# A long convolution and a spectral mixing layer on one core: the identity read with the first constants, two zero columns left out, and the first transform's tiles shared anew between two engines

## The chip, the cores and the metric

The kernel runs on one core of a Trainium2 chip. A core has TensorE (matrix products, into the banks of PSUM), VectorE (DVE in the profile), ScalarE (ACT), GpSimd (POOL) and SyncE (SP). DMA transfers are issued here by SP and POOL and carried out by 16 DMA engines. The metric is the time of one execution in device microseconds; before the change the median of three runs was 385.36 us (384.66 to 386.22).

## The reference

Two layers in a row, with x of shape (8, 5696, 128) and h of shape (5696, 128): a causal convolution along the sequence, by FFT, and then a mixing of the 64 lowest frequencies with complex 128 x 128 matrices, followed by a gated residual.

```python
# first layer
Xf = np.fft.rfft(x, n=2 * S, axis=1)
Hf = np.fft.rfft(h, n=2 * S, axis=0)
u0 = np.fft.irfft(Xf * Hf[None], n=2 * S, axis=1)[:, :S, :]
# second layer
X = np.fft.rfft(u0, axis=1)
Y = np.zeros_like(X)
Yr = Xr @ w_r - Xi @ w_i          # the first 64 modes, one matrix each
Yi = Xr @ w_i + Xi @ w_r
u = u0 + np.fft.irfft(Y, n=S, axis=1)
out = u + np.maximum(u @ w_ch, 0.0)
```

## The kernel before

The kernel is written instruction by instruction. A recorder (line 21) keeps one list for each engine; an instruction's waits come from tokens that it reads and writes, and each engine runs its own list strictly in the order in which the program adds to it. So does each DMA queue (SP's and POOL's).

**The transform.** S = 5696 is split into NQ = 89 rows of J = 64 positions. The first transform goes along the 89 rows and gives NK = 90 frequencies k, real and imaginary part: one matmul with the moving matrix `F1` of 2 * NK = 180 columns for each feature d. Of these, the imaginary parts at k = 0 and k = 89 are zero for every input. `a_tile` (line 461) makes four features: four matmuls into two PSUM banks, and then one evacuation (`evac`, line 304) of 128 x 720 values to `As` in fp16, as a multiplication by 1/64, on VectorE (line 317) or on ScalarE (line 313). 32 such tiles make `As` for one pair of batches; the same is done for h at half the width (`Ah`). The second transform (`second`, line 606, and `filter_tick`, line 486, for h) takes four k in a tick; for each k and each batch it adds two matmuls, one with the real and one with the imaginary part.

**The four passes.** The eight batches go in four pairs g_ = 0 to 3. The body of a pass has 23 ticks of four k (`tick`, line 650): second transform, products with the filter (`products`), a matmul pair W1/W2, evacuation to a slot of `Zs`/`Zt` on ScalarE, a store of the slot to the scratch `zscr` through SP's queue, and the matmuls with `G` that collect the 64 modes. In the last pass a slot is used again after eight ticks (NZL = 8): the evacuation of tick 21 writes the slot of tick 13, and so waits until the store of tick 13 has landed.

**The borders.** Between two passes all of `As` is made anew. Tiles j = 0 to 5 are spread over the last ticks (`border`, line 556: five on VectorE, one on ScalarE); tiles 6 to 31 follow in a loop (line 740). That loop takes the PSUM slots 4, 6, 0, 2 in turn, so a tile can start when the tile four places ahead of it has been evacuated. Odd tiles go to VectorE, even ones to ScalarE, the last one is halved between both. `second` of the next pass needs all 32 tiles.

**The opening.** For the first pass the tiles stand alone in a loop (line 717), with `eng=None`, which lets ScalarE and VectorE take turns; six ticks of the filter's second transform (`filter_tick`) are put between them, five of them evacuated by ScalarE and one by VectorE. `keep(16, ...)` after it is sixteen matmuls without use that keep TensorE busy. The opening cannot start before the first pair of x has been loaded through POOL's queue.

**The last pass and the tail.** While the last pass runs, a table `early` (line 557) issues the loads for the final stage at given ticks: POOL reads the weights `W`, the tables `S4b`, `S4a` and `IBs` and the first stored spectra `ZT0`, `ZT1`. At tick 14 it calls `load_id` (line 568): SP reads the 128 x 128 identity into `Id`, which lies on one of the buffers `R`. It is issued after ZY, that is after everything that read or wrote slots 8 and 9, the landing of their stores to `zscr` among it. The stores of ticks 13, 14 and so on stand behind it in SP's queue. The identity is used once, in eight transposes (line 824) in the tail, after the mixing matmuls. The tail (`u_z`, `mix`, `u_c`, from line 760) and the final stage (`u_tile`, `o_tile`) follow.

```python
early = {..., 11: lambda: load_zt(0, "gpsimd"),
         14: lambda: (load_id(), clear_zt(1)), ...}
def load_id():
    dma("sync", id_sb[:, :], bass.AP(c_w, 2 * P, [[3 * P, P], [1, P]]), "c", (), [("id",)], after=ZY)
```

Of the kernel before, what the change touches and what calls it, by code (L numbers as in the profile page):

```python
# [123 lines left out]
def bass_long_conv_fft__then__afno_spectral_mix_kernel(nc, x, h, moe_w_r, moe_w_i, moe_w_ch, out):  # L124
# [16 lines left out]
    fwd = np.exp(-2j * np.pi * np.outer(qq, kk) / (2 * NQ))  # L141
    f1 = np.zeros((P, 2 * NK))
    f1[0:NQ] = np.stack([fwd.real, fwd.imag], axis=2).reshape(NQ, 2 * NK)
    mat = np.exp(-2j * np.pi * (pp[:, None, None] * kk[None, :, None] / L + pp[:, None, None] * pp[None, None, :] / J))
# [64 lines left out]
    def take(nbytes):  # L209
# [38 lines left out]
          [at(f"Zt{i}", 1024, F16, a_g + GW * 2 + i * 2048) for i in range(NZX - NZ)]  # L248
    f1_sb = at("F1", 2 * NK, F16, take(2 * NK * 2))
    wc_sb = at("Wc", 2 * P, F16, take(2 * P * 2))  # L250
# [11 lines left out]
              (a_m2, a_g)]  # L262
    assert 2 * S + 8 * ZP <= AW * 2
    zt = [[at(f"ZT{i}{'ab'[p_]}", ZP, F16, zt_off[i][p_]) for p_ in range(2)] for i in range(NC)]
# [17 lines left out]
    c_sb = at("C", B * P, F16, a_x + 4 * S)  # L282
    id_sb = at("Id", P, F16, r_off[1])

# [14 lines left out]
    def bank(i):  # L299
        return ("bank", i)  # L300
# [45 lines left out]
    zf = x_sb[J:P, :].bitcast(F32)  # L346
    R.add("scalar", lambda e: e.copy(zf, ap(f1_sb, 2 * NK, J, P - J, 1, [[0, XW // 2]])), [("f1",)], [("xz",)])
    h_parts = [part for i in range(2) for part in (
# [67 lines left out]
    dma("sync", sg_sb[:, :], c_sg.ap(), "c", (), [("sg",)])  # L416
    dma("sync", wc_sb[:, :], bass.AP(c_w, 0, [[3 * P, P], [1, 2 * P]]), "c", (), [("wc",)])

    def mtok(k):
# [12 lines left out]
    for i in range(WARM):  # L432
        mm(pv(6 + i % 2, 0, [[1, 2 * NK]]), f1_sb[:, 0:P], f1_sb[:, :], True, True, [("f1",)], [bank(6 + i % 2)])

# [5 lines left out]
    for j in range(16):  # L440
        t = turns("h", [0, 2, 4])
        for i in range(4):
            d = 4 * j + i
            mm(pv(t + i // 2, (i % 2) * 2 * NK, [[1, 2 * NK]]),
               ap(hp_sb, 2 * J * HS, 0, P, d, [[HS, 2 * J]]), f1_sb[:, :], True, True,
               [("hz",), ("hp", d // DC), ("f1",)], [bank(t + i // 2)])
        for i in range(4 if j < 15 else 26):
            mm(pv(6 + i % 2, 0, [[1, 2 * NK]]), f1_sb[:, 0:P], f1_sb[:, :], True, True, [("f1",)], [bank(6 + i % 2)])
        evac(bass.AP(ah_sb, 4 * j, [[HW, P], [DH, 2 * NK], [2, 2], [1, 2]]),
             pv(t, 0, [[1, 2 * NK], [512, 2], [2 * NK, 2]]),  # L450
             [bank(t), bank(t + 1)], [("ah", j)], 1.0 / 64,
             eng="vector" if j in (3, 7) else "scalar")
# [8 lines left out]
    def a_tile(j, slots, eng=None):  # L461
        t = turns("s", slots) if len(slots) > 1 else slots[0]
        for i in range(4):
            d = 4 * j + i
            mm(pv(t + i // 2, (i % 2) * 2 * NK, [[1, 2 * NK]]),
               ap(x_sb, XW, 0, P, d, [[XS, 2 * J]]), f1_sb[:, :], True, True,
               XIN + XZ + [("f1",)], [bank(t + i // 2)])
        if eng == "both":
            for i, e in enumerate(("vector", "scalar")):
                evac(bass.AP(a_sb, 4 * j + 2 * i, [[AW, P], [D, 2 * NK], [1, 2]]), pv(t + i, 0, [[1, 2 * NK], [2 * NK, 2]]),  # L470
                     [bank(t + i)], [("as", j + i)], 1.0 / 64, eng=e, after=once(("hp", j), HP))
            return
        evac(bass.AP(a_sb, 4 * j, [[AW, P], [D, 2 * NK], [2, 2], [1, 2]]),
             pv(t, 0, [[1, 2 * NK], [512, 2], [2 * NK, 2]]),
             [bank(t), bank(t + 1)], [("as", j)], 1.0 / 64, eng=eng, after=once(("hp", j), HP))


    def xtok(n):
# [7 lines left out]
    def filter_tick(t, banks):  # L486
        n = len(ticks[t])
        hb = banks
        for i, k in enumerate(ticks[t]):
            for r in range(2):  # L490
                for dh in range(2):
                    mm(pv(hb[dh], i * DH, [[1, DH]]),
                       ap(m_sb, MW, J * dh, J, k * 3 * J + (J if r == 0 else 0) + dh * J, [[1, P]]),
                       ap(ah_sb, HW, J * dh, J, (2 * k + r) * DH, [[1, DH]]), r == 0, r == 1,
                       AHT + mtok(k) + [("ag", k)], [bank(hb[dh])])
# [54 lines left out]
    def load_s4(part):  # L550
# [24 lines left out]
    def keep(n, b0):  # L575
        for i in range(n):
            mm(pv(b0 + i % 2, 0, [[1, 2 * NK]]), f1_sb[:, 0:P], f1_sb[:, :], True, True, [("f1",)], [bank(b0 + i % 2)])

# [27 lines left out]
    def second(g_, t):  # L606
        sl = slot_of(g_, t)
        for i, k in enumerate(ticks[t]):
            for r in range(2):
# [231 lines left out]
    def o_tile(g_, b, r4):  # L841
# [97 lines left out]
```

## Time and profile before

| what | us |
|---|---|
| median of three runs (lowest, highest) | 385.36 (384.66, 386.22) |
| the profiled execution | 387.21 |
| its span, first to last instruction | 385.1 |
| TensorE busy | 362.4 (94%) |
| ScalarE busy | 314.3 (82%) |
| VectorE busy | 296.6 (77%) |
| GpSimd busy | 85.2 (22%) |
| granted TensorE clock, mean over the span | 0.98 |

The profile tells when each engine was busy and who ended each wait. A row of the groups gives the line of the program, the engine, the operation, out<-in, how often it ran, its busy time and mean duration in ns, and then the idle time of the engine just before it and what ended it. In a row of the timeline, the first number is the start and the second the length in us of a run of like instructions (xN); the bracket gives the idle time before it. TensorE is busy nearly throughout, but a matmul's recorded time overlaps that of the next, so the share alone does not say that TensorE is the limit. That has to be read stage by stage:

| stretch, us | stage |
|---|---|
| 0 to 27 | loads, transform of h |
| 27 to 43.5 | opening: first transform of pass 0, first ticks of the filter |
| 43.5 to 91, 107 to 147, 162 to 202, 218 to 262 | the bodies of the four passes |
| 91 to 107, 147 to 162, 202 to 218 | the three borders |
| 262 to 274 | tail: last spectra, mixing, transposes |
| 274 to 385 | final stage and output |

### The profile page before, as it was taken

To read this page: it belongs to the slowest core of one execution; us is meant where nothing else is said; L and a number is where in the kernel's file an instruction comes from. 1 tells how busy PE (TensorE), PEld (TensorE's weight loads), DVE (VectorE), ACT (ScalarE), POOL (GpSimd) and SP (SyncE) were. 2 spreads that over 40 slices of the span, in tenths; PEclk is the share of its full clock that TensorE was granted. 3 is DMA by queue.
4 is the path that set the end of the run, shared out by engine and by line. 5 is a ranking of instruction groups with operands and counts; after the bars stand their busy time and mean duration, and the time that the engine had idled before them with its cause. 6 is when DMAs were issued, how large, how long until landed. Compare 5 with 4: busy or idle time off the path is not lost.

```text
span 385.1 us, 12438 instructions
## 1 busy us (share of the span) xinstructions
PE 362.4 (94%) x5346; PEld 280.7 (73%) x5346; DVE 296.6 (77%) x336; ACT 314.3 (82%) x491; POOL 85.2 (22%) x134
## 2 busy tenths in 40 slices
PE   7989899999989999999999899978999999999994
PEld 7878766667856667756667666648789989888873
DVE  3649899988988998989999988761537767766665
ACT  8469699898989997899998899965447777688884
POOL 8812012100733311823203213307200000000000
PEclk9999999999999999999999999995799999999999
DMA  7999969977999995999995799999999999999877
GB/s 148 206 298 354 243 139 249 250 220 222 97 126 215 249 268 151 132 134 232 243 274 114 95 325 357 327 367 292 392 391 362 367 416 403 419 405 383 325 293 316
DMA packets 87137, 103.94 MB, mean 270 GB/s; under 512 B 22819, under 2 KB 72611, under 8 KB 83527
## 3 DMA queue, kind: packets, MB, share of 16 engines
q1 hardware_dynamic: 62603, 67.76, 50.7%
q0 software_dynamic: 24480, 35.40, 44.2%
q8 instruction: 42, 0.69, 0.7%
q14 instruction: 12, 0.10, 0.1%
HBM read 70.61 MB, written 51.12 MB: 316 GB/s over the span
## 4 chain that ended last, share of the span: by engine, by line
PE 76%; DMA 8%; DVE 6%; ACT 4%; POOL 3%; issue 2%; DVEq 0%; ACTq 0%; POOLq 0%
PE ps L323 76%; DMA Xr<-in_x_dram 4%; DMA zscr<-Zs 3%; DVE As L317 2%; DVE U L630 2%; POOL Xr L320 2%; ACT As L313 2%; ACT R L871 1%; POOL Hin L320 1%; DVE Xin L365 1%; DVE Hs L315 1%; ACT Zt L311 1%; ACT Zs L311 0%; DMA Hs<-Hs 0%; ACT Xs L311 0%
## 5 line engine op out<-in xcount | busy, mean ns | idle before, releaser
L323 PE MATMUL ps<-U,Wc 128*128 128x512 f16 (+1 forms) x368 | 94.4, 377 | 4.2 <-ACT Zs L311 3.7
L638 DVE TENSOR_TENSOR U<-Xs,Hs 128x2048 f16<-128x2048 f16 (+1 forms) x73 | 86.9, 1192 | 13.8 <-ACT Xs L311 13.1
L311 ACT CAST Xs<-ps 128x1024 f16<-128x1024 f32 (+1 forms) x77 | 75.1, 979 | 12.6 <-PE ps L323 7.6
L311 ACT CAST Zs<-ps 128x512 f16<-128x512 f32 (+1 forms) x132 | 69.3, 592 | 5.5 <-DMA zscr<-Zs 3.8
L872 DVE TENSOR_TENSOR O<-ps,R 128x512 f32<-128x512 f32 x81 | 52.3, 685 | 20.1 <-ACT R L871 11.2
L317 DVE TENSOR_SCALAR As<-ps 128x720 f16<-128x720 f32 x70 | 57.7, 886 | 5.2 <-PE ps L323 4.6
L871 ACT ACTIVATE R<-ps 128x512 f32<-128x512 f32 (+1 forms) x92 | 50.5, 591 | 8.5 <-PE ps L323 8.4
L323 PE MATMUL ps<-F,Xin 128*128 128x180 f16 x512 | 53.7, 249 | 3.9 <-DVE Xin L365 2.6
L323 PE MATMUL ps<-As,M 64*128 64x128 f16 x1440 | 50.3, 217 | 3.5 <-DVE U L630 2.9
L323 PEld LDWEIGHTS ps<-F,Xin 128*128 128x128 f16 x512 | 44.4, 155 | 12.6 <-DVE As L317 2.8
L323 PEld LDWEIGHTS ps<-U,Wc 128*128 128x128 f16 x368 | 28.6, 97 | 33.3 <-ACT Zs L311 7.6
L313 ACT ACTIVATE As<-ps 128x720 f16<-128x720 f32 (+1 forms) x61 | 45.7, 769 | 7.9 <-PE ps L323 6.5
L323 PE MATMUL ps<-WI,UT 128*128 128x256 f16 x360 | 51.1, 278 | 0.5 <-ACT UT L311 0.4
L311 ACT CAST UT<-ps 128x712 f16<-128x712 f32 x46 | 34.5, 752 | 19.2 <-PE ps L323 18.0
L323 PEld LDWEIGHTS ps<-As,M 64*128 64x128 f16 x1440 | 40.6, 94 | 9.7 <-DVE U L630 3.6
L323 PEld LDWEIGHTS ps<-WI,UT 128*128 128x128 f16 x360 | 39.1, 152 | 3.4 <-issue 1.8
L323 PE MATMUL ps<-IBs,C 128*128 128x356 f16 x128 | 40.3, 324 | 0.1
L320 POOL DMA_DIRECT2D Xt<-in_x_dram x40 | 21.1, 533 | 80.8 <-PE ps L323 80.3
L323 PEld LDWEIGHTS ps<-G,Zs 128*128 128x128 f16 x512 | 26.3, 97 | 14.3 <-ACT Zs L311 1.6
L638 DVE TENSOR_TENSOR U<-ps,Hs 128x2048 f16<-128x2048 f32 x15 | 34.3, 2284 | 0.0
L323 PE MATMUL ps<-G,Zs 128*128 128x128 f16 (+2 forms) x512 | 32.4, 193 | 0.0
L311 ACT CAST Zt<-ps 128x512 f16<-128x512 f32 x52 | 28.5, 624 | 0.3 <-PE ps L323 0.3
(88 smaller groups left out, 504.7 us busy)
## 6 DMA issues: line engine op xcount, KB each, us to landing
out_dram<-O SPq DMA_DIRECT2D x39, 512.0 KB, 7.6
zscr<-Zs SPq DMA_DIRECT2D x62, 256.0 KB, 7.0
zscr<-Zt SPq DMA_DIRECT2D x26, 256.0 KB, 6.8
Xt<-in_x_dram POOLq DMA_DIRECT2D x20, 320.0 KB, 7.1
W<-wscr POOLq DMA_DIRECT2D x4, 1024.0 KB, 8.2
M<-cM POOLq DMA_DIRECT2D x5, 720.0 KB, 16.9
ZT0a<-zscr SPq DMA_DIRECT2D x3, 1024.0 KB, 8.8
Hs<-Hs SPq DMA_DIRECT2D x44, 64.0 KB, 6.3
```

Source lines behind the costliest of these rows:

```text
L311: R.add(e, lambda h_: h_.copy(dst, src), reads, writes, after=after)
L313: R.add(e, lambda h_: h_.activation(dst, src, COPY, scale=scale), reads, writes, after=after)
L315: R.add(e, lambda h_: h_.tensor_copy(dst, src), reads, writes, after=after)
L317: R.add(e, lambda h_: h_.tensor_scalar_mul(dst, src, scale), reads, writes, after=after)
L320: R.add(eng, lambda h_: h_.dma_start(dst, src), reads, writes, ring=ring, after=after)
L323: R.add("tensor", lambda h_: h_.matmul(o, l, r, start=st, stop=sp), reads, writes)
L365: R.add("vector", lambda e: e.tensor_copy(bass.AP(x_sb, i * XN * XS, [[XW, NQ], [XS, XN], [1, D]]), src), list(toks) + XZ, [("xin", i)])
L630: R.add("vector", lambda e, b=b, s_=s_: e.tensor_tensor(bass.AP(u_s[i], b * 512, [[2048, P], [1024, 2], [1, n * D]]), s_, hv, MULT), [tok, ...
L638: R.add("vector", lambda e: e.tensor_tensor(uv, src, hv, MULT), bk + [("h", t, 0), ("h", t, 1, 0), ("h", t, 1, J)], [("u", i)])
L871: R.add("scalar", lambda e: e.activation(rv, src_r, RELU), bk, [("r", i % NR)], after=once(("r", i % NR), G_ALL + XTT + [("y", 0), ("y", 1 ...
L872: R.add("vector", lambda e: e.tensor_tensor(ov, src_u, rv, ADD), bk + [("r", i % NR)], [key + (h_,)], after=once(key, old))
```

## The change

- `F1` loses the two zero columns: NF = 178 columns instead of 180. Each first-transform matmul streams 178 columns, an evacuation moves 128 x 712 values, and the second transform makes one matmul instead of two at k = 0 and at k = 89 (`parts_of`). The groups in `As` shift by one (`group`), and the last 256 bytes of a row of `As` are free.
- `Id` is put there, and its read is issued by SP at the start, right behind `Wc`. `load_id` and its place at tick 14 are gone; the first use of a buffer `R` no longer waits for the readers of `Id`.
- In the opening the engines follow a written order (`SHARE`), with the last tile halved: 15 tiles on VectorE, 16 on ScalarE and one on both, where each had 16. In the three border loops the order is A V A V A V A V A over nine tiles and then again: of the 25 whole tiles ScalarE gets 14 (13 before) and VectorE 11 (12 before). Tiles 0 to 5 of a border keep their engines.
- Filling the rows 64 to 127 of `Xin` copies column 1 of `F1`, which was zero in all rows and now holds values in rows 64 to 88; x is written over those rows later.

```diff
-    f1 = np.zeros((P, 2 * NK))
-    f1[0:NQ] = np.stack([fwd.real, fwd.imag], axis=2).reshape(NQ, 2 * NK)
+    NF = 2 * NK - 2
+    f1 = np.zeros((P, NF))
+    f1[0:NQ] = np.delete(np.stack([fwd.real, fwd.imag], axis=2).reshape(NQ, 2 * NK), [1, 2 * NK - 1], axis=1)
...
-    id_sb = at("Id", P, F16, r_off[1])
+    id_sb = at("Id", P, F16, a_as + (2 * NK - 1) * D * 2)
...
     dma("sync", wc_sb[:, :], bass.AP(c_w, 0, [[3 * P, P], [1, 2 * P]]), "c", (), [("wc",)])
+    dma("sync", id_sb[:, :], bass.AP(c_w, 2 * P, [[3 * P, P], [1, P]]), "c", (), [("id",)])
...
-        evac(bass.AP(a_sb, 4 * j, [[AW, P], [D, 2 * NK], [2, 2], [1, 2]]),
-             pv(t, 0, [[1, 2 * NK], [512, 2], [2 * NK, 2]]),
+        evac(bass.AP(a_sb, D + 4 * j, [[AW, P], [D, NF], [2, 2], [1, 2]]),
+             pv(t, 0, [[1, NF], [512, 2], [NF, 2]]),
              [bank(t), bank(t + 1)], [("as", j)], 1.0 / 64, eng=eng, after=once(("hp", j), HP))
...
+    def group(k, r):
+        return 2 * k + r if k else 1
+
+    def parts_of(k):
+        return (0,) if k in (0, NK - 1) else (0, 1)
...
-            for r in range(2):
+            for r in parts_of(k):
                 for b in range(2):
                     col = k * 3 * J + (J if r == 0 else 0) + b * J
                     mm(pv(sl + b, i * D, [[1, D]]),
                        ap(m_sb, MW, J * b, J, col, [[1, P]]),
-                       ap(a_sb, AW, J * b, J, (2 * k + r) * D, [[1, D]]), r == 0, r == 1,
+                       ap(a_sb, AW, J * b, J, group(k, r) * D, [[1, D]]), r == 0, r == parts_of(k)[-1],
                        AST + mtok(k), [bank(sl + b)])
...
-             14: lambda: (load_id(), clear_zt(1)),
+             14: lambda: clear_zt(1),
...
-    def load_id():
-        dma("sync", id_sb[:, :], bass.AP(c_w, 2 * P, [[3 * P, P], [1, P]]), "c", (), [("id",)], after=ZY)
-
...
+    SHARE = [V if c_ == "V" else A for c_ in "VAVAAVAVAVAVAVAVAVAAVVAVAVAVAVA"]
     for j in range(32):
-        a_tile(j, FOUR)
+        a_tile(j, FOUR, "both" if j == 31 else SHARE[j])
...
-                a_tile(j, [(4, 6, 0, 2)[(j - 7) % 4] if j > 6 else 0], "both" if j == 31 else V if j % 2 else A)
+                a_tile(j, [(4, 6, 0, 2)[(j - 7) % 4] if j > 6 else 0], "both" if j == 31 else (A, V)[(j - 6) % 9 % 2])
...
-        R.add("scalar", lambda e: e.activation(rv, src_r, RELU), bk, [("r", i % NR)], after=once(("r", i % NR), G_ALL + XTT + [("y", 0), ("y", 1), ("id",)]))
+        R.add("scalar", lambda e: e.activation(rv, src_r, RELU), bk, [("r", i % NR)], after=once(("r", i % NR), G_ALL + XTT + [("y", 0), ("y", 1)]))
```

The same replacement of 2 * NK by NF is made for h (`Ah`), in `filter_tick`, and in the matmuls without use (the warm-up and `keep`).

More of the change, by code (lines that the diff above doesn't have):

```diff
@@ L248, in bass_long_conv_fft__then__afno_spectral_mix_kernel @@
           [at(f"Zt{i}", 1024, F16, a_g + GW * 2 + i * 2048) for i in range(NZX - NZ)]
-    f1_sb = at("F1", 2 * NK, F16, take(2 * NK * 2))
+    f1_sb = at("F1", NF, F16, take(NF * 2))
     wc_sb = at("Wc", 2 * P, F16, take(2 * P * 2))
@@ L262, in bass_long_conv_fft__then__afno_spectral_mix_kernel @@
               (a_m2, a_g)]
-    assert 2 * S + 8 * ZP <= AW * 2
+    assert 2 * S + 8 * ZP <= (2 * NK - 1) * D * 2 and 2 * XC * XB * 2 <= (2 * NK - 1) * D * 2
     zt = [[at(f"ZT{i}{'ab'[p_]}", ZP, F16, zt_off[i][p_]) for p_ in range(2)] for i in range(NC)]
@@ L346, in bass_long_conv_fft__then__afno_spectral_mix_kernel @@
     zf = x_sb[J:P, :].bitcast(F32)
-    R.add("scalar", lambda e: e.copy(zf, ap(f1_sb, 2 * NK, J, P - J, 1, [[0, XW // 2]])), [("f1",)], [("xz",)])
+    R.add("scalar", lambda e: e.copy(zf, ap(f1_sb, NF, J, P - J, 1, [[0, XW // 2]])), [("f1",)], [("xz",)])
     h_parts = [part for i in range(2) for part in (
@@ L432, in bass_long_conv_fft__then__afno_spectral_mix_kernel @@
     for i in range(WARM):
-        mm(pv(6 + i % 2, 0, [[1, 2 * NK]]), f1_sb[:, 0:P], f1_sb[:, :], True, True, [("f1",)], [bank(6 + i % 2)])
+        mm(pv(6 + i % 2, 0, [[1, NF]]), f1_sb[:, 0:P], f1_sb[:, :], True, True, [("f1",)], [bank(6 + i % 2)])
     DC = DH // 2
@@ L443, in bass_long_conv_fft__then__afno_spectral_mix_kernel @@
             d = 4 * j + i
-            mm(pv(t + i // 2, (i % 2) * 2 * NK, [[1, 2 * NK]]),
+            mm(pv(t + i // 2, (i % 2) * NF, [[1, NF]]),
                ap(hp_sb, 2 * J * HS, 0, P, d, [[HS, 2 * J]]), f1_sb[:, :], True, True,
@@ L447, in bass_long_conv_fft__then__afno_spectral_mix_kernel @@
         for i in range(4 if j < 15 else 26):
-            mm(pv(6 + i % 2, 0, [[1, 2 * NK]]), f1_sb[:, 0:P], f1_sb[:, :], True, True, [("f1",)], [bank(6 + i % 2)])
-        evac(bass.AP(ah_sb, 4 * j, [[HW, P], [DH, 2 * NK], [2, 2], [1, 2]]),
-             pv(t, 0, [[1, 2 * NK], [512, 2], [2 * NK, 2]]),
+            mm(pv(6 + i % 2, 0, [[1, NF]]), f1_sb[:, 0:P], f1_sb[:, :], True, True, [("f1",)], [bank(6 + i % 2)])
+        evac(bass.AP(ah_sb, DH + 4 * j, [[HW, P], [DH, NF], [2, 2], [1, 2]]),
+             pv(t, 0, [[1, NF], [512, 2], [NF, 2]]),
              [bank(t), bank(t + 1)], [("ah", j)], 1.0 / 64,
@@ L464, in a_tile @@
             d = 4 * j + i
-            mm(pv(t + i // 2, (i % 2) * 2 * NK, [[1, 2 * NK]]),
+            mm(pv(t + i // 2, (i % 2) * NF, [[1, NF]]),
                ap(x_sb, XW, 0, P, d, [[XS, 2 * J]]), f1_sb[:, :], True, True,
@@ L469, in a_tile @@
             for i, e in enumerate(("vector", "scalar")):
-                evac(bass.AP(a_sb, 4 * j + 2 * i, [[AW, P], [D, 2 * NK], [1, 2]]), pv(t + i, 0, [[1, 2 * NK], [2 * NK, 2]]),
+                evac(bass.AP(a_sb, D + 4 * j + 2 * i, [[AW, P], [D, NF], [1, 2]]), pv(t + i, 0, [[1, NF], [NF, 2]]),
                      [bank(t + i)], [("as", j + i)], 1.0 / 64, eng=e, after=once(("hp", j), HP))
             return
-        evac(bass.AP(a_sb, 4 * j, [[AW, P], [D, 2 * NK], [2, 2], [1, 2]]),
-             pv(t, 0, [[1, 2 * NK], [512, 2], [2 * NK, 2]]),
+        evac(bass.AP(a_sb, D + 4 * j, [[AW, P], [D, NF], [2, 2], [1, 2]]),
+             pv(t, 0, [[1, NF], [512, 2], [NF, 2]]),
              [bank(t), bank(t + 1)], [("as", j)], 1.0 / 64, eng=eng, after=once(("hp", j), HP))
+    def group(k, r):
+        return 2 * k + r if k else 1
+    def parts_of(k):
+        return (0,) if k in (0, NK - 1) else (0, 1)
     def xtok(n):
@@ L493, in filter_tick @@
                        ap(m_sb, MW, J * dh, J, k * 3 * J + (J if r == 0 else 0) + dh * J, [[1, P]]),
-                       ap(ah_sb, HW, J * dh, J, (2 * k + r) * DH, [[1, DH]]), r == 0, r == 1,
+                       ap(ah_sb, HW, J * dh, J, group(k, r) * DH, [[1, DH]]), r == 0, r == parts_of(k)[-1],
                        AHT + mtok(k) + [("ag", k)], [bank(hb[dh])])
@@ L576, in keep @@
         for i in range(n):
-            mm(pv(b0 + i % 2, 0, [[1, 2 * NK]]), f1_sb[:, 0:P], f1_sb[:, :], True, True, [("f1",)], [bank(b0 + i % 2)])
+            mm(pv(b0 + i % 2, 0, [[1, NF]]), f1_sb[:, 0:P], f1_sb[:, :], True, True, [("f1",)], [bank(b0 + i % 2)])
     LC, LM, LH = 2, 3, 6
@@ L608, in second @@
         for i, k in enumerate(ticks[t]):
-            for r in range(2):
+            for r in parts_of(k):
                 for b in range(2):
```

## The prediction

> **What bounds the kernel now.** I read the timeline of a border first, since the change moves tiles there, then the chain of waits, the wait lists and SP's timeline around tick 14 of the last pass.
>
> The third border, engine by engine:
>
> ```profile
> 207.41 9.41 PE L323 MATMUL ps<-F,Xin 128*128 128x180 f16 x92 [0.25 <-ACT As L313]
> ...
> 207.98 9.52 DVE L317 TENSOR_SCALAR As<-ps 128x720 f16<-128x720 f32 x12 [0.19 <-PE ps L323]
> ...
> 208.29 9.27 ACT L313 ACTIVATE As<-ps 128x720 f16<-128x720 f32 x12 [0.28 <-PE ps L323]
> ...
> 217.65 1.07 PE L323 MATMUL ps<-As,M 64*128 64x128 f16 x32 [0.21 <-ACT As L313]
> ```
>
> VectorE runs eleven whole tiles and a half one without a pause. Three tiles in a row elsewhere take 2.54 us at 0.90 for one, so its step is 0.82 (0.8145 from the single starts). ScalarE keeps the same pace only because tiles alternate: alone it is faster, as in the transform of h, where (5.41 - 0.78) / 7 = 0.66 us a tile:
>
> ```profile
> 18.90 5.41 ACT L313 ACTIVATE Ah<-ps 128x720 f16<-128x720 f32 x8 [0.46 <-PE ps L323]
> ...
> 22.97 2.04 PEld L323 LDWEIGHTS ps<-F 128*128 128x128 f16 x26
> 23.04 2.18 PE L323 MATMUL ps<-F 128*128 128x180 f16 x26
> ```
>
> The second pair of rows gives TensorE's own pace: 2.04 / 26 = 0.0785 us (0.0775 between starts), 0.31 for a tile's four. So a border goes at 0.407 us a tile, set by VectorE.
>
> Next, the longest stop of TensorE after the opening, in the chain of waits and then in the list of waits (us in total, times, longest):
>
> ```profile
> 247.65 0.20 ACT Zs L311
> 247.86 13.02 DMA zscr<-Zs
> 260.88 0.02 issue
> ...
> 260.96 0.60 ACT Zs L311
> ```
>
> ```profile
> ACT Zs L311 <- DMA zscr<-Zs: 3.8, 1, 3.8
> PE ps L323 <- ACT Zs L311: 3.7, 1, 3.7
> ...
> SPq L320 <- DMA zscr<-Zt: 3.4, 1, 3.4
> ```
>
> The store of tick 13 takes 13.02 us to land; tick 21's evacuation waits for its slot, and TensorE stands still from 257.92 to 261.60. The last row is SP waiting for a landing before the identity's load. SP's rows there:
>
> ```profile
> 239.97 4.00 SPq L320 DMA_DIRECT2D zscr<-Zs  x3
> 247.48 0.33 SPq L320 DMA_DIRECT2D Id<-cW  x1
> 247.86 3.37 SPq L320 DMA_DIRECT2D zscr<-Zs  x3
> ```
>
> Last, what the stop does to the clock (columns: length, busy time of PE, PEld, DVE, ACT, POOL, granted clock, DMA share, GB/s):
>
> ```profile
> 255.00:258.00 3.00, 2.92 (x31) 1.46 (x27) 1.75 (x2) 2.17 (x5) 0.00 (x0) 1.00 1.03 358
> 258.00:262.00 4.00, 0.40 (x2) 0.28 (x3) 0.00 (x0) 1.04 (x3) 0.00 (x0) 0.80 0.90 274
> 262.00:264.00 2.00, 2.00 (x28) 1.87 (x27) 0.38 (x2) 1.46 (x5) 1.76 (x4) 0.50 1.21 344
> ```
>
> 0.80 over four us means half clock from 260.4; the trace's clock record has it from 260.40 to 274.05, 13.65 us.
>
> **The change part by part.**
>
> *Border order and 178 columns.* I followed the 26 tiles of the loop one by one with five numbers of the trace: four matmuls 0.31; evacuation at the earliest 0.565 after a tile's first matmul (206.00 to 206.57); steps of 0.8145 (VectorE) and 0.668 (ScalarE); results out after 0.90 and 0.78; a slot taken again 0.055 after its evacuation (205.95 to 206.00). With the old order this gives the last evacuation at 217.53; the trace has 217.56. With the new order and widths (712 of 720 values: steps 0.806 and 0.661) it gives 217.14: -0.39 us. The narrower tiles alone, in the old order, give 217.43. Why not more: the engines alone would need 4 x 0.806 = 3.22 and 5 x 0.661 = 3.31 for nine tiles, 0.368 a tile, a gain of 25 x (0.407 - 0.368) = 1.0; but two ScalarE tiles in a row wait for one another, and the tile four places on waits for their slots. A UT row of the same width (128x712, ScalarE 752 ns, VectorE 892) shows no penalty for that width. Three borders: -1.17 (bounds -0.3 and -3.0).
>
> *Opening.* The same with the filter's ticks between gives the last evacuation at 42.69 instead of 43.04 (trace 43.39). The sixteen `keep` matmuls, 1.24 us, cover part of that: they end at 42.82. I take -0.25 (0 to -0.35).
>
> *Identity read early.* One issue of 0.33 us on SP, where nothing follows before 32.9. Its 128 packets of 256 bytes (18 ns each by the packet record) lie, eight to a DMA engine, in front of loads of h and x whose landing at 26.24 starts the opening: 8 x 18 = 0.14 us at most by this. I take +0.1 (0 to 0.14).
>
> *Two matmuls fewer in a pass's first tick.* They run as a pair at 0.056 us a pair, and VectorE's first product waits for them: 4 x 0.056 = 0.22, with 0.03 for the filter -0.25. In tick 22 ScalarE and VectorE are the limit: 0.
>
> *Identity gone from tick 14.* SP's 3.4 us of waiting go. What was queued behind: the stores of ticks 13 and 14, whose evacuations end at 245.5 and 246.5 (four in 2.06 us from 244.47); they can be issued 2.3 and 1.8 us earlier. But the landing is not set by issue: packet by packet, the slowest DMA engine is done with the stores of ticks 10 to 12 only at 250.7, and from then until 260.2 alternates, one small packet against one of 8,192 or 5,874 bytes of ZT1, S4a and IBs (Id's eight stand 0.32 us apart there). Without Id, the store has those eight turns and the few empty ones before 252.4, on an engine busy until 260.2 anyway; 12 of its 32 packets were left then. So between 0.2 (the same packets later, 8 x 0.024 us) and the whole 3.7 plus the half clock (if the early issue brings it ahead of ZT1 on that engine). I take -0.5, nearest to the packet rows, and keep the half clock; its cost is worked out below.
>
> *R's dropped wait* concerns transposes over by 271.1, 17 us before the first R (288.06): 0.
>
> Sum: -1.17 - 0.25 + 0.1 - 0.25 - 0.5 = -2.07. The profiled execution took 387.21 with a span of 385.1, 2.1 lying around it; it would become 385.1, the span 383.0. It stands 1.85 above the median of 385.36, so for the median I forecast **383.3**. The bodies pass the gain on because all their engines are full (39.63 of 41.00 us TensorE, 38.66 VectorE, 38.36 ScalarE in the first), and the transfers are issued by ticks; after 274 TensorE is busy to the end.
>
> **The rivals.**
>
> *A: the clock stays up.* With TensorE's stop shortened to 3.2 us or less, the half clock may not be granted. For it: it is the one drop inside the kernel, and follows the one stop over 2 us. Against: the drop came although TensorE worked for 0.9 of the 3.41 us before it (256.98 to 260.40). Price: 48 small products of the tail at 0.0735 instead of 0.039 us, 1.7; six wide ones at 0.297 instead of 0.150 and sixteen small ones, 1.5; mixing and transposes about 1: 4 us. Time 379; with the stop gone as well, 376. [...]
>
> *B: the engines alone set the border*, if the waits for slots are milder than my tile-by-tile rule: -3.0 instead of -1.17, 381.5. Against: the rule hits the old border within 0.03.
>
> *C: the DMA engines do not move along.* If the loads of the last pass are backlogged from its start, the landing at 260.9 stays where it is, and all that is gained before is spent waiting: only the 0.5 at the stop remains, 384.9. For: DMA shares of 0.9 and more from 231 on. Against: tenths 5 and 7 in the slices from 212 to 231, so the backlog begins inside the pass.
>
> [...]
>
> **How the numbers follow.** Forecast 0.48, A 0.22, B 0.08, C 0.14, D 0.08. About 0.5%, 1.9 us, is what a measurement of this kernel can tell from no change: faster is below 383.43, slower above 387.29. Faster: A, B and just over half of the forecast, 0.56. Slower: half of D and what I have not seen, 0.07. The rest, 0.37, is within. Range 378.5 to 386.0: it holds the forecast, B, C and the nearer half of A, 0.81 in all; the forecast's own is 382.3 to 384.2.
>
> **What would show it.** Right: in each border the stretch from the first evacuation of tile 6 to the second transform's first matmul falls from 11.1 to about 10.7 us; SP's row of the stores after 239.97 has no pause over 3 us; TensorE's stop near 256 is 2.9 to 3.5 us and half clock follows for 13.7 us; `Xin` filled within 0.15 us of 26.95. Wrong: a granted clock of 1.0 from 255 to 275 (A), borders of 10.1 us (B), a stop of 4.5 us or more (C, D), or a store of tick 13 that lands within 8 us of its issue, which would overthrow my account of the alternation.

## The result and the profile after

The changed kernel is slower: 386.77 us, median of 22 runs (383.79 to 388.97), against 383.06 us for the kernel before (22 runs, 381.70 to 387.74). The ratio is 1.0066, 95% interval 1.0043 to 1.0089. Medians here take in all runs, ratios leave out those more than 1.5% above the fastest of their kernel, so the two can differ a little. The execution of before that the prediction was worked from, 387.21 us, was one of its longest; that of after, 386.69 with a span of 384.4, is an ordinary one.

The border did what it was to do. The timeline of the third border in the profile after (start, length, engine, line, operation, out<-in, how often, idle time before):

```profile
207.35 8.98 PE L324 MATMUL ps<-F,Xin 128*128 128x178 f16 x92 [0.26 <-ACT As L314]
207.93 9.08 DVE L318 TENSOR_SCALAR As<-ps 128x712 f16<-128x712 f32 x11 [0.20 <-PE ps L324]
...
208.23 8.96 ACT L314 ACTIVATE As<-ps 128x712 f16<-128x712 f32 x13 [0.28 <-PE ps L324]
...
217.25 1.01 PE L324 MATMUL ps<-As,M 64*128 64x128 f16 x30 [0.26 <-ACT As L314]
```

VectorE's row took 9.52 us before and takes 9.08; the second transform makes 30 matmuls in its first tick, not 32. But the stop at the end of the last pass is still there. The chain of waits after, from 243 us on, and two rows of the waits between 255 and 275 us (us in total, times, longest):

```profile
242.97 3.15 PE ps L324 x41
246.12 13.94 DMA zscr<-Zs
260.06 0.02 issue
...
260.84 1.17 PE ps L324 x19
262.01 0.06 issue
262.07 5.67 PE ps L324 x152
```

```profile
ACT Zs L312 <- DMA zscr<-Zs: 2.4, 1, 2.4
PE ps L324 <- ACT Zs L312: 2.3, 1, 2.3
```

It is the store of tick 14 now, not 13, that lands 13.94 us after its issue; tick 22 waits for its slot, and TensorE stops for 2.32 us. The store of tick 13 landed at 250.17, 5.03 us after its issue. In the profile before these were 13.02 us (tick 13) and a stop of 3.68.

A second profile of the kernel before, taken with the experiments (382.10 us, near its median), has no stop there at all. So the stop of 3.68 us belongs to one execution of that kernel and not to each. Set against the second profile, most of the loss is found in two places, the body of the last pass and the end:

| stretch, us | before (382.10) | after (386.69) |
|---|---|---|
| start to the last pass's first matmul | 217.11 | 217.25 |
| body of the last pass, to the first mixing matmul | 42.35 | 44.82 |
| mixing, transposes, first products, to the first output matmul | 22.77 | 23.19 |
| output matmuls, first to last | 91.95 | 92.01 |
| last matmul to the end | 5.79 | 7.09 |
| span | 379.97 | 384.36 |

### The profile page after: what moved, and what is told of

It is laid out like the page before. It is cut to its first block, busy times and chain, and to the rows that moved or that the text cites. A ratio compares the mean times of both kernels' runs of the same rounds, so it can differ in the third digit from the quotient of the medians.

```text
span 384.4 us, 12403 instructions
## 1 busy us (share of the span) xinstructions
PE 358.6 (93%) x5326; PEld 277.9 (72%) x5326; DVE 294.9 (77%) x333; ACT 314.0 (82%) x495; POOL 84.8 (22%) x134
## 4 chain that ended last, share of the span: by engine, by line
PE 68%; DMA 12%; ACT 8%; DVE 5%; POOL 3%; issue 2%; DVEq 0%; POOLq 0%; ACTq 0%
PE ps L324 68%; ACT As L314 6%; DMA Xt<-in_x_dram 4%; DMA Xr<-in_x_dram 4%; DMA zscr<-Zs 4%; DVE As L318 2%; DVE U L635 2%; POOL Xr L321 2%; ACT R L877 1%; POOL Hin L321 1%; DVE Xin L366 1%; DVE Hs L316 1%; DMA Hs<-Hs 0%; PE ps L830 0%; ACT Xs L312 0%
## 5 line engine op out<-in xcount | busy, mean ns | idle before, releaser
L318 DVE TENSOR_SCALAR As<-ps 128x712 f16<-128x712 f32 (+1 forms) x67 | 55.1, 873 | 5.7 <-PE ps L324 4.0
L324 PE MATMUL ps<-F,Xin 128*128 128x178 f16 x512 | 51.9, 249 | 5.1 <-DVE Xin L366 3.7
L314 ACT ACTIVATE As<-ps 128x712 f16<-128x712 f32 (+1 forms) x65 | 45.5, 762 | 7.3 <-PE ps L324 6.7
```

The lines of the kernel that those rows point to most:

```text
L314: R.add(e, lambda h_: h_.activation(dst, src, COPY, scale=scale), reads, writes, after=after)
L318: R.add(e, lambda h_: h_.tensor_scalar_mul(dst, src, scale), reads, writes, after=after)
L324: R.add("tensor", lambda h_: h_.matmul(o, l, r, start=st, stop=sp), reads, writes)
```

## The experiments

Besides timed runs I use two records of the trace that the page only sums up. One gives each DMA's landing on each of the 16 engines, so that its median and its slowest engine can be told apart. The other holds every packet, those of a queue named instruction among them, which this row of the DMA view of after counts (packets, MB, share of 16 engines):

```profile
q8 instruction: 42, 0.69, 0.7%
```

They are 42 reads of 16,384 bytes. TensorE's records hold 10,762 instructions (10,802 before): 5,326 matmuls, as many weight loads and 110 waits. 42 times 256 is 10,752, so my estimate from these counts is that the reads fetch TensorE's program, one for 256 instructions, 64 bytes each. I call this a block, and number blocks by their reads from 0.

### Which part of the change costs the time

Three theories: Q, the loss lies in the DMA queues at the end of the last pass; X, transfers of x ahead of the borders; W, the width of 178 itself. Four kernels: the kernel before again; the narrowing alone (178 columns, 40 instructions of TensorE fewer); the narrowing with the early identity; the narrowing with the new orders, and the identity at tick 14 as before.

The narrowing is the part of the change with `NF`, `group` and `parts_of`, beginning with

```diff
+    NF = 2 * NK - 2
...
+    def parts_of(k):
+        return (0,) if k in (0, NK - 1) else (0, 1)
```

The identity and the orders are its lines

```diff
+    dma("sync", id_sb[:, :], bass.AP(c_w, 2 * P, [[3 * P, P], [1, P]]), "c", (), [("id",)])
...
+        a_tile(j, FOUR, "both" if j == 31 else SHARE[j])
...
+                a_tile(j, [(4, 6, 0, 2)[(j - 7) % 4] if j > 6 else 0], "both" if j == 31 else (A, V)[(j - 6) % 9 % 2])
```

> The kernel before, unchanged, for a profile of a usual execution (the first one stood 4 us above the median of 22 runs) and for the scatter of the comparison. All theories: ratio 1.000 within 0.3%. Theory Q (the loss lies at the end of the last pass, in the DMA queues behind the identity's load): TensorE's stop near 258 us is shorter here than the 3.7 us of the first profile, or half clock follows for fewer than 13.7 us, and the span is near 381. Theory X (the loss lies in the transfers of x ahead of the borders): no wait of 0.9 us on a landing of x before the second and third border.

> 178 columns and the fewer matmuls alone: identity at tick 14 as before, old order of the tiles. Theory Q: -0.1% to -0.3% (narrower tiles, 0.1 us a border, and 0.25 us for the first ticks). Theory X: about 0. Theory W (the width of 178 columns itself costs): slower by 0.5% or more.

> 178 columns and the early identity, old order of the tiles. Theory Q: this carries the loss, slower by 0.5 to 1% against before, with TensorE's stop at tick 22 of the last pass instead of tick 21. Theory X: within 0.2%, since the borders are as before. Theory W: as in the run with the columns alone.

> 178 columns and the new order in opening and borders, identity at tick 14 as before. Theory Q: faster than before by 0.2 to 0.5%. Theory X: slower by about 0.5%, with waits on landings of x before the second and third border as in the changed kernel (1.0 and 0.9 us). Theory W: slower as with the columns alone.

| kernel | median, us | ratio to before (95%) |
|---|---|---|
| before again | 382.33 | 0.9966 (0.9938 to 0.9993) |
| narrowing alone | 386.24 | 1.0068 (1.0037 to 1.0098) |
| with identity | 389.82 | 1.0135 (1.0093 to 1.0177) |
| with orders | 387.10 | 1.0086 (1.0052 to 1.0121) |

The first row shows that 0.3% between two equal kernels means nothing. X is out: the kernel with the orders has no wait of 0.9 us ahead of its second and third border. Q expected that kernel to be faster, and it is slower. The narrowing with the identity is slower still, on six runs; I didn't follow that up. The narrowing alone has the whole loss, as W has it; yet its tiles are faster: it begins the last pass at 216.25, 0.86 us earlier than the kernel before. It loses 1.44 us to a stop for a slot at 257 us and more in the mixing. TensorE's timeline there:

```profile
262.96 1.01 PE L324 MATMUL ps<-XT,W 128*128 128x16 f16 x27
267.36 1.26 PE L324 MATMUL ps<-XT,W 128*128 128x16 f16 x37 [3.39 <-issue]
```

In the middle of 64 equal matmuls TensorE stands still for 3.39 us, and the bracket names no semaphore. In the kernel with the orders it is 3.59 us. Both stops lie after the same 7,617 instructions of TensorE, and both end 1.3 us after the read of block 28 has landed (266.07 and 264.81). The kernel with the orders stops again, 1.10 us, after 8,897 instructions: 7,617 and five times 256. So I take it that TensorE waited for its own program. If block 28 begins with instruction 7,617, the narrowing alone began block 27 at 258.95 us, and the read of block 28 only 6.2 us later; in the profile after it began 1.8 us later, and there was no stop. What the narrowing changes, beside the tiles, is where the program stands in its blocks: 20 matmuls with 20 weight loads fewer, 36 of the 40 instructions ahead of the last pass's second tick.

### Moving the program, not the work

Theory F: the place of the blocks makes the loss. Theory P: what is gained brings the issues forward but not the DMA engines. One kernel gives the kernel before the place of the changed one; one gives the changed kernel the place of the one before; two load ZT1 later.

In the kernel before, 36 of the 92 warm-up matmuls become 18 of twice the width:

```diff
-    WARM = 92
+    WARM = 74
...
     for i in range(WARM):
+        wn = 2 if i < 18 else 1
-        mm(pv(6 + i % 2, 0, [[1, 2 * NK]]), f1_sb[:, 0:P], f1_sb[:, :], True, True, [("f1",)], [bank(6 + i % 2)])
+        mm(pv(6 + i % 2, 0, [[1, wn * 2 * NK]]), f1_sb[:, 0:P], ap(f1_sb, 2 * NK, 0, P, 0, [[0, wn], [1, 2 * NK]]), True, True, [("f1",)], [bank(6 + i % 2)])
```

In the changed kernel 18 are added, or ZT1 is moved, or both:

```diff
-    WARM = 92
+    WARM = 110
```

```diff
-             15: lambda: load_zt(1, "gpsimd"),
...
+             19: lambda: load_zt(1, "gpsimd"),
```

> The kernel before, with 36 instructions of TensorE fewer at the start and no other work changed: of the 92 warm-up matmuls without use, 36 are joined two by two into 18 of twice the width. In the last pass TensorE's program then stands 36 instructions earlier in its blocks, as it does with 178 columns. Theory F (TensorE waits for its own program: the trace shows 42 reads of 16,384 bytes, one for 256 instructions; the stops of 3.39 and 3.59 us before the mixing matmuls lie at the same instruction, 7,617, and end 1.3 us after the 29th such read): a stop of 1 to 3.5 us in the mixing stage where the kernel before has none, ratio 1.004 to 1.009. Theory P (what is gained earlier brings the issues of stores and loads forward, but not the DMA engines, and stores of ticks 13 and 14 come to lie behind ZT1, S4a and IBs): nothing is gained earlier here, so no change, ratio 0.997 to 1.003, no stop in the mixing stage.

> The changed kernel with 18 warm-up matmuls more (110 in place of 92), 1.4 us inside TensorE's wait of 2.3 us for h. Its program then stands in the last pass, block by block, where it stood before the change. Theory F: the loss goes, ratio to the kernel before 0.995 to 1.001 (the changed kernel has 1.0066). Theory P: no change from the changed kernel, 1.004 to 1.009, with a stop of 2 to 3 us near 258 in most executions.

> The changed kernel with the load of ZT1 issued at tick 19 in place of tick 15, behind S4a and IBs. Theory P: the stores of ticks 13 to 17 no longer have ZT1's packets of 8,192 bytes ahead of them; the stores of ticks 13 and 14 land within 8 us of their issue, there is no stop of over 1 us near 258, half clock there is 2 windows (6.8 us) or fewer, ratio to the kernel before 0.988 to 0.996. Theory F: the fetch of TensorE's program is only helped where it lay behind ZT1; ratio 1.002 to 1.008.

> The two edits before together: 18 warm-up matmuls more and ZT1 loaded at tick 19. If both theories hold, no stop over 1 us after 230 us and ratio 0.986 to 0.994, 0.002 or more below the better one of the two alone. If only P holds, as with ZT1 alone within 0.002; if only F, as with the 18 matmuls alone within 0.002.

| kernel | median, us | ratio to before (95%) |
|---|---|---|
| before, 36 instructions fewer | 389.08 | 1.0132 (1.0089 to 1.0175) |
| changed, 18 matmuls more | 381.86 | 0.9952 (0.9916 to 0.9988) |
| changed, ZT1 at tick 19 | 384.28 | 1.0021 (0.9990 to 1.0051) |
| changed, both | 381.63 | 0.9957 (0.9928 to 0.9986) |

In the times, F holds in both directions. The kernel before does the same work and loses 1.3%, more than the 0.4 to 0.9% that I expected; the changed kernel does 18 useless matmuls more and gains 1.1%. That it is also 0.5% faster than the kernel before is little beyond the 0.3% between two equal kernels. The chain of the changed kernel with 18 matmuls more, to be read against that of after:

```profile
257.53 1.23 ACT Zs L312 x3
258.76 0.04 issue
258.81 1.03 PE ps L324 x19
259.83 0.20 issue
260.04 5.25 PE ps L324 x152
```

No store is in it, and the mixing runs through. With ZT1 later the slots no longer stop TensorE either, but block 28 does, for 2.47 us; that is P's part, and it is worth nothing once the blocks are in place (0.9957 beside 0.9952).

My expectation for the shifted kernel before was wrong in one point, though: its stop is not in the mixing. Its chain shows the store of tick 13 again, and SP's timeline shows what held that up:

```profile
249.73 10.23 DMA zscr<-Zs
259.95 0.02 issue
```

```profile
239.96 3.44 SPq L320 DMA_DIRECT2D zscr<-Zs  x3
249.35 0.33 SPq L320 DMA_DIRECT2D Id<-cW  x1
249.73 2.35 SPq L320 DMA_DIRECT2D zscr<-Zs  x3
```

The identity's load waits for the store of tick 9, which lands at 249.33, 8 us later than in the undisturbed profile of before (241.35). So the place of a block seems to act in a second way, through the DMA engines. The landings by engine point to it in the first ticks of the last pass; the records do not name the engine, so that the late one is the one with the read is argued, not shown:

| profile | block 24 read at | third load of W issued | it lands, median / slowest engine | store of tick 2, median / slowest |
|---|---|---|---|---|
| before (382.10) | 223.8 | 224.6 | 230.5 / 231.0 | 231.1 / 231.7 |
| before (387.21) | 226.4 | 225.2 | 231.5 / 234.0 | 232.2 / 237.5 |
| changed, 18 more | 224.5 | 225.2 | 230.9 / 231.5 | 231.7 / 232.2 |
| before, 36 fewer | 225.4 | 224.6 | 230.3 / 234.0 | 230.9 / 237.0 |
| changed | 225.5 | 224.7 | 230.9 / 233.0 | 231.5 / 236.2 |
| narrowing alone | 224.3 | 223.7 | 229.4 / 232.2 | 230.0 / 233.9 |

Where the read starts ahead of the load's issue, the slowest engine is 0.5 us behind the median one. Where it starts behind it, 2.1 to 3.7 us, and the store behind the load 3.9 to 6.1.

The first two rows are the same program. By the count above TensorE began block 23 at 223.5 in the one execution and at 224.0 in the other, and the read of block 24 began 0.4 and 2.4 us later. So the place in the program does not fix the time of a read: the kernel before, left as it is, falls on either side, and its execution of 387.21 has the late engine, and the stop (3.68 us) for the store of tick 13, that the shifted one has.

Ten ticks later SP issues the store of tick 14 and POOL, 0.11 to 0.12 us later, the first part of ZT1. The timeline of after, and then that of the kernel before (382.10):

```profile
246.12 1.83 SPq L321 DMA_DIRECT2D zscr<-Zs  x1
...
246.24 0.54 POOL L321 DMA_DIRECT2D ZT1a<-zscr  x1 [0.82 <-PE ps L324]
```

```profile
246.02 0.36 SPq L320 DMA_DIRECT2D zscr<-Zs  x1
...
246.13 0.54 POOL L320 DMA_DIRECT2D ZT1a<-zscr  x1 [0.82 <-PE ps L323]
```

In the kernel before the issue takes 0.36 us, and the store lands at 250.91, ahead of ZT1's first part (253.4, 7.3 us after its issue). After, the issue takes 1.83 us, to 247.95; the store of tick 10 ends on its slowest engine only at 248.11 (246.64 before). What held the issue up is not shown. ZT1's first part lands at 254.5, 8.3 us after its issue, and the store at 260.06.

### Where the blocks may stand

The two ways are now called F1 (TensorE waits for a block) and F2 (the read makes one DMA engine late). One kernel is to move W's third load past the read; three add narrow matmuls to move the blocks by 36, 64 and 96 matmuls, where by the estimate above 128 with their weight loads make a block.

```diff
-    early = {3: lambda: load_w(2), 5: lambda: load_w(3), 8: lambda: load_s4(1),
+    early = {4: lambda: load_w(2), 5: lambda: load_w(3), 8: lambda: load_s4(1),
```

The narrow matmuls stand behind the warm-up, 36 or 64, and for the 96 another 32 stand ahead of the opening:

```diff
+    for i in range(64):
+        mm(pv(6 + i % 2, 0, [[1, 8]]), f1_sb[:, 0:P], f1_sb[:, 0:8], True, True, [("f1",)], [bank(6 + i % 2)])
...
+        for i in range(32 if j == 15 else 0):
+            mm(pv(6 + i % 2, 0, [[1, 8]]), f1_sb[:, 0:P], f1_sb[:, 0:8], True, True, [("f1",)], [bank(6 + i % 2)])
```

> The changed kernel with the third load of W at tick 4 in place of tick 3; TensorE's program is not touched. Theory F2 (the read of a 16,384-byte block of TensorE's program sits on one of the 16 DMA engines; where it falls just behind the issue of W's third load, that engine is 2 to 4 us late with it, and the stores behind come 5 us late): the block now lies ahead of the load, whose slowest engine ends within 1 us of the median one (2.1 us in the changed kernel), the store of tick 14 lands within 8 us of its issue (13.9), and the stop of 2.3 us near 258 is gone; but the stop for block 28 in the mixing stage may take its place, as in three other kernels, so ratio 1.000 to 1.006. Theory F1 (the blocks count only where TensorE waits for one): the stop near 258 stays at 2 to 3 us, ratio 1.004 to 1.009.

> The changed kernel with 36 narrow matmuls (8 columns) more behind the warm-up, inside TensorE's wait for h: every block begins 72 instructions of the program earlier than in the changed kernel, 36 earlier than in the kernel with 18 more. F1 and F2: the read in the first ticks of the last pass comes near 222.5, ahead of W's third load, and its last block is asked for 5 us earlier at the end; ratio 0.993 to 0.998, like the kernel with 18 more, and no more than 6.0 us from the last matmul to the end (7.1 in the changed kernel). If what helped there was 1.4 us of additional work at the start and not the blocks: 0.5 to 1.0 is lost by its absence, ratio 1.002 to 1.008.

> As before with 64 narrow matmuls, half a block. F2: the read falls near 219 to 220, while W's second load runs and 4 us ahead of the third; the engine has caught up by then: ratio 0.993 to 0.999. F1: block 28 is asked for some 92 instructions before the first slot that can stop TensorE, and has landed long before it is needed: no stop in the mixing stage, ratio 0.993 to 0.999. If only the length of the program counts, the same as with 18 or 36 within 0.002.

> As before with 96 narrow matmuls (32 of them in the wait for x). A block is 128 matmuls with their weights, so the blocks stand as with 32 matmuls fewer than the changed kernel has: F2: the read falls near 226 to 227, behind W's third load, whose slowest engine is 2 us or more behind the median one; the stores of ticks 13 and 14 land more than 8 us after their issue, ratio 1.004 to 1.014, slower than with 64 by 0.007 or more. If a longer program were the help and not the place of the blocks: 0.993 to 0.999.

| changed kernel with | median, us | ratio to before (95%) |
|---|---|---|
| 0 matmuls more | 386.77 | 1.0066 (1.0043 to 1.0089) |
| 18 | 381.86 | 0.9952 (0.9916 to 0.9988) |
| 36 | 381.72 | 0.9961 (0.9930 to 0.9993) |
| 64 | 383.67 | 0.9994 (0.9959 to 1.0028) |
| 96 | 386.70 | 1.0076 (1.0039 to 1.0113) |
| 0, W's third load at tick 4 | 385.96 | 1.0051 (1.0022 to 1.0080) |

The time goes down and up again within one block, while the program only gets longer: it is the place, not the length. With 64 the ratio came out just above what I expected. With 96 TensorE stops in the mixing again, and the stop has moved as it must, from the 27th matmul of the last 64 to the 59th, by 128 - 96 = 32:

```profile
264.57 1.98 PE L324 MATMUL ps<-XT,W 128*128 128x16 f16 x59
268.25 0.31 PE L324 MATMUL ps<-XT,W 128*128 128x16 f16 x5 [1.70 <-issue]
```

The load at tick 4 missed its aim. It was issued at 224.9 with the read at 224.7 to 226.2, side by side again; its slowest engine was 3.1 us behind, and the stop near 257 stayed, 2.25 us.

The reads did not come where F2 expected them, though the times mostly did. With 36 the read came at 224.9, not near 222.5, 0.6 us behind the load's issue, and yet the slowest engine was only 0.9 us late. With 64 it came at 225.6, not near 219 to 220, 1.0 us ahead of the load; its profile, of that kernel's longest run (387.39), has a stop of 2.33 us near 260, since the store of tick 13 ends on one engine 10 us behind the median. With 96 it came at 224.9, 1.7 us behind the load, with an engine 2.9 us late, and the stores of ticks 13 and 14 landed 14.8 and 13.4 us after their issue, as expected.

Over all sixteen profiles, those of the next section among them, a read that starts 0.5 to 2.1 us behind the load's issue goes with an engine 2.1 to 3.7 us late in ten of eleven; the eleventh is the one with 36. One that starts 0.7 us or more ahead goes with 0.2 to 0.8 in all four; the load at tick 4, with its read 0.2 ahead, has 3.1. A late engine alone does not cost the time: with 18 matmuls more and ZT1 at tick 19 it is 2.7 us late, and the time is 381.63.

### Moving the load, not the program

The changed kernel, and then the kernel before:

```diff
-    early = {3: lambda: load_w(2), 5: lambda: load_w(3), 8: lambda: load_s4(1),
+    early = {5: lambda: load_w(2), 7: lambda: load_w(3), 8: lambda: load_s4(1),
```

```diff
-    early = {3: lambda: load_w(2), 5: lambda: load_w(3), 8: lambda: load_s4(1),
+    early = {2: lambda: load_w(2), 5: lambda: load_w(3), 8: lambda: load_s4(1),
```

> The changed kernel with W's third and fourth loads at ticks 5 and 7 in place of 3 and 5; TensorE's program is not touched, so its blocks are read where they were (about 8.3 us into the last pass). Theory F2: the block near 225.5 now lies 2 us ahead of W's third load (near 227.8), whose slowest engine ends within 1.2 us of the median one (2.1 in the changed kernel); the stores of ticks 2 and 3 land by 233 (236.2 and 236.8 there). What the later loads do to the stores of ticks 13 and 14, and block 28 in the mixing stage, are left as they are, so the time may stay between 0.998 and 1.008. If the slow engine has another cause than the read beside the load: its lag behind the median stays at 2 us or more.

> The kernel before with W's third load at tick 2 in place of tick 3; TensorE's program and its blocks are untouched. Theory F2: the read near 223.8 now falls behind the issue of that load (near 222.6) instead of ahead of it; the slowest engine is 1.5 us or more behind the median one (0.5 in the kernel before), the stores behind it come 3 to 6 us late, and the time goes up as with the shifted program: ratio 1.003 to 1.012. If the place of the block counts only for TensorE's own wait: ratio 0.997 to 1.003.

The engines did as F2 has it, in one profile each. In the changed kernel with later loads the third load's slowest engine was 0.2 us behind the median one, and that of the two stores issued behind it 0.3 and 0.5; the next one, behind the fourth load, had 4.1. The stores of ticks 2 and 3 landed at 228.1 and 228.8, but they were now issued ahead of the load, so this tells nothing. In the kernel before with the earlier load it was 3.3 us behind, and the stores of ticks 1 and 2 ended on it 7 us behind their medians. The times are less plain. The first stays slow, 1.0055 (1.0005 to 1.0104) without the six longest of its twelve runs, and a median of 388.20 with them; in its profile, of a run of 388.87, the fourth load and S4b now crowd together, the store of tick 14 takes 1.75 us to issue and lands after 14.6 us all the same, TensorE stops 3.00 us for that slot, and block 28 stops the mixing for 2.51 us. The second is 1.0017 (0.9977 to 1.0057), which fits either theory; five of its twelve runs are at 382.0 to 383.3 and seven at 385.3 to 387.1. So a block read beside a load goes with a late engine here too. That the second edit made it late is not shown, since the kernel before has 0.5 us in one profile and 2.5 in the other without any edit. And that place alone doesn't decide the time.

### The end

The last block, 41, is read near the end. It begins 13 x 256 instructions behind the 7,617 at which block 28 begins, at 10,945, and so holds none of the 10,762 instructions. Where it was read late, as in the changed kernel (read at 376.3), the last output's slowest engine comes 1.84 us behind the median one, and from the last matmul to the end it takes 7.09 us. In the eight profiles of kernels with 18, 36, 64 or 96 matmuls more, or of the kernel before with its program as it was, no block is read between 374 us and the end of the span, and the end takes 5.2 to 5.8 us; in the other eight one is read between 374 and 379 us, and it takes 6.6 to 7.6. This is what the sixteen profiles show side by side; no edit of its own tests that the read is the cause.

## Why the prediction was wrong

- *Borders, -1.17 in all: right.* From `Xin`'s first matmul to the second transform the three borders took 16.44, 16.37 and 16.35 us before and take 16.12, 15.96 and 15.99: -1.09. The narrowing alone has 16.35, 16.22 and 16.21; the forecast for it was -0.10 each, and it is -0.09, -0.15 and -0.14.
- *Opening, -0.25: right.* 16.44 became 16.21. In two of the ten profiles with the new order, with half clock from about 28 us on, for 3.4 us, it is 17.4; the prediction did not reckon with that.
- *Identity read early, +0.1: not to be told.* `Xin`'s first matmul is at 27.07 (27.10 and 27.07 in the two profiles of before), but it lies between 26.90 and 27.39 in the sixteen profiles.
- *Two matmuls fewer in the first tick, 0.056 us a pass: right in size.* The bodies of the second and third pass take 39.02 us in the changed kernel with 18 matmuls more and ZT1 later (39.07 and 39.09 before). In the profile after they take 39.62 and 39.55, since TensorE waits 0.99 and 0.91 us for x at their ends; no other profile with the new orders has such a wait, so I count it to that execution, without having tested it.
- *Identity gone from tick 14, -0.5, half clock kept: the account failed.* By the prediction's own test, the store of tick 13 landing within 8 us (5.03) overthrows its alternation of packets. The stop of 3.7 us that it reckoned with is not there in every execution: the profile at 382.10 still has the identity at tick 14 and no stop. What the term is worth is not shown, since no run takes the identity away with the blocks in place and all else equal.
- *"The bodies pass the gain on ... after 274 TensorE is busy to the end": the step that failed.* The bodies' engines were as full as it says, but the last pass waits for a store besides (2.32 us in the profile after), in other profiles, as I read them, for TensorE's own program (1.10 to 3.59 us), and at the end the last output comes late; the gain came through only with the blocks in place. Between the changed kernel's profile and that with 36 matmuls more (span 379.20), the body of the last pass accounts for 44.82 - 42.31 = 2.51 us, the end for 7.09 - 5.24 = 1.85, the mixing for 0.37, all that is ahead for 0.46. The medians differ by 386.77 - 381.72 = 5.05.
- *What the sum lacked.* It had the 40 missing instructions as time, -0.25 us, and not as a shift of all that follows in the program. With the shift taken back the ratio is 0.9952, with twice as much 0.9961; the forecast, 383.3 to 385.36, was 0.9947. So a term of 4 to 5 us was missing. That the rest agrees is in part luck: the identity's term is in it without its account, 64 matmuls more give 0.9994, and two equal kernels came 0.3% apart.
- *The rivals.* D, at 0.08, stood for 386.6 us, with half clock prolonged by a longer stop. That is the measured time, but the runs do not show D's term: in the profile after the stop is shorter, 2.32 us for 3.68, and half clock too, 10.24 us for 13.65. C, engines that do not move along, has a part, since ZT1 at tick 19 gave 0.45% back; the part goes when the blocks are moved. A and B did not come about.

Half clock was no large part either. These two stretches, of the kernel before (382.10) and of after, have the columns of the windows shown in the prediction:

```profile
258.00:262.00 4.00, 3.73 (x100) 3.49 (x98) 2.94 (x2) 3.25 (x4) 4.00 (x4) 0.96 1.12 379
262.00:264.00 2.00, 2.00 (x64) 2.00 (x62) 0.45 (x1) 0.48 (x1) 2.00 (x4) 0.50 1.02 408
```

```profile
258.00:262.00 4.00, 1.58 (x26) 1.12 (x23) 0.32 (x2) 1.43 (x4) 1.33 (x3) 0.94 1.03 316
262.00:264.00 2.00, 1.94 (x54) 1.96 (x54) 0.82 (x1) 2.00 (x1) 2.00 (x3) 0.50 1.00 243
```

The clock halves in both at 261.6 or 261.7, with a stop and without one, for 6.8 us before and 10.2 after; the whole stretch from the mixing to the first output matmul differs by 23.19 - 22.77 = 0.42 us.

## What to carry to other kernels

An edit that adds or removes instructions moves everything behind it in the engine's program (36 instructions fewer cost the kernel before 1.3%); where the DMA engines are as full as here (a share of 1.03 from 230 to 285 us in the profile of after), shift the program by a few useless instructions in a wait, in both directions, before the edit is blamed or praised. An idle time that ends with "issue" in the middle of equal instructions can be a wait for the program itself (3.39 and 3.59 us here); what spoke for it was the instruction number, 7,617 in both, and 5 x 256 more at the next such stop. One profile is one execution: a stop that a sum rests on should be seen in a second one, and set against the spread of the runs.

The best of the kernels run keep the change and add 18 or 36 useless matmuls at the start: 381.86 and 381.72 us, 0.9952 and 0.9961 of the kernel before. Against the changed kernel that is clear; against the kernel before it is little more than the 0.3% between two equal kernels.

## What was unexpected in the hardware

- A block of 16,384 bytes is one packet of 0.88 to 1.72 us (the profile of after, from 230 us on), and the 42 are 0.7% of the DMA time; yet their place moved the time by 1.3% in the kernel before and by 1.1% in the changed one. That a block holds 256 instructions of TensorE is the estimate above, from 42 reads for 10,762 records; two stops of one profile, 5 x 256 instructions apart, agree with it. TensorE stood still for 1.10 to 3.59 us where I count such a wait, in five of sixteen profiles.
- With blocks counted as above, each of the 657 reads after the first ones, in the sixteen profiles, starts between 1.1 us before and 7.8 us after TensorE begins the block ahead of it, 2.8 in the median.
- One late engine of 16 stood ahead of a long landing: in the profile of after the store of tick 2 lands at 231.5 on the median engine and at 236.2 on the slowest, and the store of tick 14 lands 13.94 us after its issue, in place of 4.89 in the kernel before (382.10). That the one led to the other is argued, not shown.
- Half clock came without a long stop: 261.7 to 268.5 in the kernel before (382.10), with TensorE busy 3.73 of the 4 us from 258 on. This trace shows no idle time of TensorE over 0.2 us between 250 and 262 us, and with 18 matmuls more TensorE is busy without a pause from 260.04 to the drop at 264.0. What brings half clock on is not shown.
- Open remains why an engine falls 2 to 4 us behind beside a read that itself takes 1.67 us in the profile of after and 1.18 in that of before (387.21).
